# Retention attention and a gated feed-forward layer on one core: the first load on two queues, the last unit and the last output rows in two parts, and a new table of priority shifts

## The chip, the cores and the metric

The kernel runs on one core of a Trainium2 chip. A core has five engines that run side by side, each through its own list of instructions in order: PE (TensorE, matrix products), DVE (VectorE), ACT (ScalarE), POOL (GpSimd) and SP (SyncE, which here only issues transfers). Engines wait for each other by semaphores. Transfers are issued by SP or ACT and carried by 16 DMA engines. The metric is device time in microseconds (us), less is better.

## The reference, cut to what matters

```python
# q, k, v: (4, 8, 768, 64); per head: decayed attention in blocks, with a carried state
intra = einsum('bhic,bhjc->bhij', qb, kb) * Dmask       # lam ** (i - j), lower triangle
out   = einsum('bhij,bhjd->bhid', intra, vb) + einsum('bhid,bhde->bhie', qb * lam_pow, kv_state)
kv_state = lam_block * kv_state + einsum('bhsd,bhse->bhde', kb * rev_pow, vb)
# x: (3072, 512), heads side by side
xn = x / sqrt(mean(x * x) + 1e-6) * rms_g
g  = xn @ w_gate                                          # 512 x 1536
y  = (g * sigmoid(g) * (xn @ w_val)) @ w_out              # 1536 x 512
```

All tensors are float32.

## The kernel before, in words

The 3072 tokens are six groups `m` of 512 (four tiles `t` of 128), the heads four pairs `p`, and the 1536 hidden columns twelve slices `f` of 128. For each group and pair PE computes scores (`pa`, L509), sums for the state (`pst`, L542), the mix of values (`po`, L574) and the state's part (`po`, L585); ACT scales K with the decay (L519), DVE multiplies the scores with the mask (L529) and carries the state (L555, L557), POOL scales Q (L533). A group's rows are then normalised: row sums on PE (`pss`), a power on POOL, spread by PE (`pr`), a product on DVE (L716), a 16-bit cast on ACT (L721) and the rest of it on DVE or POOL (L724).

A unit `u` is one slice of one group in the feed-forward layer. It makes gate and value products (`pg` and `pv`, L763, in the first groups; `pa` and `pb`, L938, seven products instead of eight, later), SiLU on ACT, `mul_sums` on DVE (L1004), `high` on ACT (a 16-bit cast, L1028) and `low` on DVE (the rest, L1035). Then `out_product` adds three products to each of the four accumulators `acc` (L782 to L784). After the last slice `out_rows` scales an accumulator into a tile `o` and `send` stores it.

float32 weights arrive as raw 64-bit words (`raw_gv` gate and value, `raw_o` output rows) and are converted on the chip: lift (ACT, L220), shifts (DVE, L229 and L232), squares (ACT, L442) whose sums are a product on PE (`pn`, L447), and the 16-bit high and low parts (`wg`, `wv`, L465 and L469). The first weight tile lands in `partial`.

Constants `cs` (lambda and rms_g) come in one small transfer. DVE makes decay masks and powers from them (scans, L156 and L161), and `gmax`, the largest rms_g, which PE spreads (`pmax`, L185).

All order is written by a planner. Every step is given an engine, a cost, a due time `at` in units and what it reads and writes; `SHIFTS` adds an amount to the due time of the steps that it names by number; `Plan.run` then plays the steps through on a clock of its own and emits them in the order that comes out, engine by engine, loads and stores (on SP) included. Where that clock leaves PE idle by more than 0.8 in the beginning, `busy` puts unread products there (`unread`, L144). Loads of Q, K, V and of gate and value weights share four buffers, tag `in`, so each waits until an older tile is no longer used; `pending` is the order in which they are asked for.

Of the kernel before, what the change touches and what calls it, by code (L numbers as in the profile page):

```python
# [17 lines left out]
P = 128  # L18
G = 512
# [4 lines left out]
def retention_swiglu_kernel(  # L24
# [50 lines left out]
    nc.sync.dma_start(cs, consts)  # L75
# [6 lines left out]
    def load_qkv(m, p):  # L82
        t = stage.tile([P, 4, GC, P], F32, tag="in", name=f"qkv_{m}_{p}", bufs=4)
        for i in range(2):
            queue = nc.scalar if m == p == i == 0 else nc.sync
            queue.dma_start(
                t[:, 2 * i : 2 * i + 2],
                qkv[m, p, :, 2 * i : 2 * i + 2].rearrange("p a (c i) -> p a c i", c=GC),
            )
        loaded[m, p] = [t[:, i] for i in range(4)]  # L90
# [699 lines left out]
    def out_rows(m, f, t, kept, half):  # L790

        acc = done_accs.pop((m, f, t))
# [13 lines left out]
        if m == NG - 1 and t == GC - 1:  # L806

            o = tmp.tile([P, DM], F32, tag="t", name=f"o_{m}_{t}")
            left, right = slice(0, DM // 2), slice(DM // 2, DM)
            copy(o[:, left], acc[:, left], False)  # L810
            nc.sync.dma_start(rows_[:, left], o[:, left])
            copy(o[:, right], acc[:, right], True)
            nc.scalar.dma_start(rows_[:, right], o[:, right])
            return
# [13 lines left out]
    def send(m, t):  # L828
        rows_, o = outs.pop((m, t))
        nc.sync.dma_start(rows_, o)  # L830
# [112 lines left out]
    class Hidden:  # L943
# [59 lines left out]
        def mul_sums(self):  # L1003
            nc.vector.scalar_tensor_tensor(  # L1004
                self.sg, self.val, cv[:, self.f : self.f + 1], self.sg, ALU.mult, ALU.mult
# [15 lines left out]
        def high(self):  # L1021
            if self.half:
# [3 lines left out]
            else:  # L1026
                self.hh = hp.tile([P, G], F32R, tag="hh", name=f"hh_{self.m}_{self.f}")
            nc.scalar.copy(self.hh, self.sg)  # L1028

        def low(self):  # L1030
# [319 lines left out]
    def out_steps(u, h, ats):  # L1350
# [4 lines left out]
        for t, at in enumerate(ats):  # L1355
            r = [f"hh{u}", weights] + ([] if h.half else [f"hl{u}"])
# [7 lines left out]
            ends = m == NG - 1 and t == GC - 1  # L1364
            tag = "t" if ends else "o" if t < GC - 1 else "w"
            r = [f"{acc}_{t}"] + ([f"partial:{t}"] if m == 0 else []) + (["ik"] if h.half else [])
            step("DVE" if m == 0 or t % 2 == 0 else "ACT", 0.74, at - 0.5, out_rows, m, f, t, m == 0, h.half,
                 r=r, w=[f"o{m}_{t}"], new=[(f"o{m}_{t}", tag)])
            if not ends:
                step("ST", 0.05, at, send, m, t, r=[f"o{m}_{t}"], w=[f"sent{m}_{t}"], lasts=4.0)  # L1370
# [69 lines left out]
    def arrive_steps():  # L1440
# [3 lines left out]
        step("LD", 3.4, -9, arrive, w=["cs"])  # L1444
        step("LD", 0.1, -9, arrive)
        for p in range(NP):
            for c in ("qK", "kv"):
                step("LD", 1.45, -9, arrive, w=[f"q0_{p}:{x}" for x in c])
# [114 lines left out]
    def strassen(u, h):  # L1563
# [25 lines left out]
        step("DVE", 0.42, u - 1, h.sum_val, 1, 1, r=[b, "kept0:1"], w=["kept1:1"])  # L1589
        step("DVE", 0.78, u - 0.9, h.mul_sums, r=["kept1:0", "kept1:1", "cv"], w=[f"sg{u}:0", f"sg{u}:1"])  # L1590
        tag = ("hh", "hl")[f % 2]
# [23 lines left out]
    def load_steps():  # L1615
# [204 lines left out]
```

## Time and profile before

| what | us |
|---|---|
| median of 3 runs (lowest to highest) | 660.43 (660.37 to 660.57) |
| the profiled execution | 659.59 |
| its span, first to last instruction | 657.8 |
| PE busy | 650.3 (99%) |
| DVE busy | 425.0 (65%) |
| ACT busy | 335.5 (51%) |
| POOL busy | 151.3 (23%) |
| last store issued, from the span's start | 654.50 |

The profile is of one execution. Times in it count from the span's start. A row of instructions gives start, duration, engine, line, operation, output and input tiles (numbers of buffers left out), shapes, and in brackets how long the engine stood idle before and what ended that. An x with a number counts records; a float32 product leaves two records. A PE record lasts longer than the step to the next start, because products overlap. Line numbers are those of the kernel before; in the kernel after, the same code stands 3 to 10 lines lower (L509 becomes L512, L763 becomes L766, L782 becomes L785).

### The profile page before, as it was taken

To read this page: it belongs to the slowest core of one execution; us is meant where nothing else is said; L and a number is where in the kernel's file an instruction comes from. 1 tells how busy PE (TensorE), PEld (TensorE's weight loads), DVE (VectorE), ACT (ScalarE), POOL (GpSimd) and SP (SyncE) were. 2 spreads that over 40 slices of the span, in tenths; PEclk is the share of its full clock that TensorE was granted. 3 is DMA by queue.
4 is the path that set the end of the run, shared out by engine and by line. 5 is a ranking of instruction groups with operands and counts; after the bars stand their busy time and mean duration, and the time that the engine had idled before them with its cause. 6 is when DMAs were issued, how large, how long until landed. Compare 5 with 4: busy or idle time off the path is not lost.

```text
span 657.8 us, 12390 instructions
## 1 busy us (share of the span) xinstructions
PE 650.3 (99%) x5049; PEld 442.4 (67%) x5049; DVE 425.0 (65%) x823; ACT 335.5 (51%) x674; POOL 151.3 (23%) x133
## 2 busy tenths in 40 slices
PE   9999999999999999999999999999999999999997
PEld 8845655554665556677767777777777777777774
DVE  6798898779987666866574434487443488443333
ACT  3795867658754553455454434445444335433332
POOL 2201250001475654477220011003010102000000
PEclk9999999999999999999999999999999999999999
DMA  8818654411013010112100311100230000000001
GB/s 322 338 48 316 239 210 162 162 64 59 8 64 126 24 45 1 65 66 65 65 2 1 127 67 65 65 2 1 73 122 1 1 2 1 33 33 1 1 1 64
DMA packets 14313, 51.13 MB, mean 78 GB/s; under 512 B 1712, under 2 KB 1968, under 8 KB 12848
## 3 DMA queue, kind: packets, MB, share of 16 engines
q1 hardware_dynamic: 13968, 49.69, 20.8%
q8 instruction: 39, 0.64, 0.4%
q10 hardware_dynamic: 288, 0.66, 0.4%
q14 instruction: 18, 0.15, 0.1%
HBM read 44.05 MB, written 6.29 MB: 77 GB/s over the span
## 4 chain that ended last, share of the span: by engine, by line
PE 96%; DVE 2%; ACT 1%; issue 0%; POOL 0%; DVEq 0%; POOLq 0%
PE pa L938 19%; PE pb L938 14%; PE acc L782 10%; PE pv L763 10%; PE pg L763 9%; PE acc L784 9%; PE acc L783 9%; PE pa L509 4%; PE po L574 4%; PE po L585 3%; PE pst L542 2%; PE unread L144 1%; PE pss L630 1%; DVE hh L1035 1%; PE pr L663 0%; DVE sg L1004 0%
## 5 line engine op out<-in xcount | busy, mean ns | idle before, releaser
L986 ACT COPY tx<-pa 128x256 f32<-128x256 f32 x144 | 53.6, 372 | 136.4 <-PE pa L938 135.7
L784 PE MATMUL acc<-wo,hh 128*128 128x512 f16 (+1 forms) x288 | 110.3, 383 | 0.0
L783 PE MATMUL acc<-wo,hh 128*128 128x512 f16 (+1 forms) x288 | 110.2, 383 | 0.0
L990 DVE TENSOR_TENSOR tx<-pb,tx 128x256 f32<-128x256 f32 x96 | 40.8, 425 | 73.6 <-PE pb L938 65.2
L782 PE MATMUL acc<-wo,hh 128*128 128x512 f16 x216 | 82.3, 381 | 0.7 <-DVE hh L1035 0.7
L938 PEld LDWEIGHTS <-wo 128*128 128x128 f16 x576 | 56.1, 98 | 26.6 <-issue 1.3
L994 DVE TENSOR_TENSOR sg<-pb,tx 128x256 f32<-128x256 f32 x48 | 20.3, 424 | 77.7 <-ACT tx L986 77.6
L763 PE MATMUL pv<-x,wv 128*128 128x512 f16 x288 | 69.5, 379 | 0.0
L763 PE MATMUL pg<-x,wg 128*128 128x512 f16 x288 | 69.0, 380 | 0.0
L938 PEld LDWEIGHTS <-wg 128*128 128x128 f16 x576 | 56.4, 98 | 16.1
L938 PEld LDWEIGHTS <-wv 128*128 128x128 f16 x576 | 56.3, 98 | 6.9 <-issue 0.2
L1028 ACT CAST hh<-sg 128x512 f16<-128x512 f32 (+1 forms) x72 | 44.5, 618 | 31.2 <-DVE sg L1004 16.4
L533 POOL TENSOR_TENSOR qkv<-qkv,pw 128x512 f32<-128x512 f32 x24 | 31.3, 1303 | 101.9 <-PE pa L509 67.5
L763 PEld LDWEIGHTS <-wg 128*128 128x128 f16 x288 | 26.1, 98 | 33.5 <-issue 3.6
L763 PEld LDWEIGHTS <-wv 128*128 128x128 f16 x288 | 26.7, 98 | 32.3 <-issue 2.8
L1035 DVE TENSOR_TENSOR hh<-sg,hh 128x512 f16<-128x512 f32 x54 | 42.3, 784 | 4.7 <-ACT hh L1028 2.2
L1004 DVE SCALAR_TENSOR_TENSOR sg<-tx,cv,sg 128x512 f32<-128x512 f32 x48 | 38.3, 797 | 5.0
L938 PE MATMUL pb<-tx,wo 128*128 128x256 f16 x288 | 39.3, 273 | 0.6 <-DVE tx L990 0.6
L938 PE MATMUL pa<-x,wv 128*128 128x256 f16 x288 | 39.3, 273 | 0.0
L938 PE MATMUL pa<-tx,wo 128*128 128x256 f16 x288 | 39.3, 273 | 0.0
L938 PE MATMUL pb<-x,wg 128*128 128x256 f16 x288 | 39.3, 273 | 0.0
L938 PE MATMUL pa<-x,wg 128*128 128x256 f16 x288 | 39.3, 273 | 0.0
(180 smaller groups left out, 1151.8 us busy)
## 6 DMA issues: line engine op xcount, KB each, us to landing
qkv<-in_qkv_dram SPq DMA_DIRECT2D x47, 512.0 KB, 4.9
raw_gv<-in_weights_dram SPq DMA_DIRECT2D x11, 1024.0 KB, 7.4
raw_o<-in_weights_dram SPq DMA_DIRECT2D x12, 512.0 KB, 3.7
out_dram<-o SPq DMA_DIRECT2D x23, 256.0 KB, 2.1
partial<-in_weights_dram SPq DMA_DIRECT2D x2, 512.0 KB, 11.9
qkv<-in_qkv_dram ACTq DMA_DIRECT2D x1, 512.0 KB, 4.6
out_dram<-o SPq DMA_DIRECT2D x1, 128.0 KB, 1.7
out_dram<-o ACTq DMA_DIRECT2D x1, 128.0 KB, 2.4
```

The source lines that it names most:

```text
L509: nc.tensor.matmul(self.pa[j][:, c, :], self.kT[r, c, :], self.qT[r, c, :], start=True, stop=True,)
L533: eng.tensor_mul(self.qT, self.qT, pw[:, p : p + 1, :].broadcast_to([P, GC, P]))
L763: nc.tensor.matmul(ps, w[:, kk, :], x[:, kk, :], start=i == kk == 0, stop=i == 2 and kk == NK - 1,)
L782: nc.tensor.matmul(acc, hl[:, ts_], oh, start=first, stop=False)
L783: nc.tensor.matmul(acc, hh[:, ts_], ol, start=False, stop=False)
L784: nc.tensor.matmul(acc, hh[:, ts_], oh, start=False, stop=last)
L938: nc.tensor.matmul(ps, w(ow, k), x(ox, k), start=first and i == k == 0, stop=i == 2 and k == 1, skip_group_check=True,)
L986: nc.scalar.copy(self.kept[:, i], self.pa)
L990: nc.vector.tensor_add(self.val[:, half], self.pb, self.kept[:, i])
L1004: nc.vector.scalar_tensor_tensor(self.sg, self.val, cv[:, self.f : self.f + 1], self.sg, ALU.mult, ALU.mult)
L1028: nc.scalar.copy(self.hh, self.sg)
L1035: nc.vector.tensor_sub(self.hl, self.sg, hh)
```

## The change

1. **First load.** The first half (Q and K) of pair 0 of group 0 was one transfer on ACT's queue; it becomes two, token tiles 0 and 1 on ACT's queue and 2 and 3 on SP's. `cs` moves from the front of SP's queue to the second place on ACT's, and the other half (K and V) from SP's queue to the third place on ACT's.
2. **Order of loads.** Group 1's second pair is asked for ahead of the second weight tile, and later loads shift.
3. **Last unit.** `mul_sums`, `high` and `low` of the last unit work in two halves of 256 tokens, so that accumulators 0 and 1 wait for the first half only.
4. **Last rows.** The last output tile was made half by DVE and half by ACT, and sent by SP and by ACT; now DVE makes both halves in two small tiles, and SP sends both. Tile 2 of the last group moves from DVE to ACT (`scalar_copies`).
5. **Planner.** A new table of shifts, new costs of the first arrivals, and fewer unread products: the planned idle time is divided by 0.4 and not by 0.24.

```diff
     cs = const.tile([P, NC], F32, name="cs")
-    nc.sync.dma_start(cs, consts)
...
-        for i in range(2):
-            queue = nc.scalar if m == p == i == 0 else nc.sync
-            queue.dma_start(
-                t[:, 2 * i : 2 * i + 2],
-                qkv[m, p, :, 2 * i : 2 * i + 2].rearrange("p a (c i) -> p a c i", c=GC),
-            )
+        rows_ = qkv[m, p].rearrange("p a (c i) -> p a c i", c=GC)
+        if m == p == 0:
+            nc.scalar.dma_start(t[:, :2, : GC // 2], rows_[:, :2, : GC // 2])
+            nc.sync.dma_start(t[:, :2, GC // 2 :], rows_[:, :2, GC // 2 :])
+            nc.scalar.dma_start(cs, consts)
+            nc.scalar.dma_start(t[:, 2:], rows_[:, 2:])
+        else:
+            for i in range(0, 4, 2):
+                nc.sync.dma_start(t[:, i : i + 2], rows_[:, i : i + 2])
...
-    pending = [(load_qkv, 1, 0), (load_gv, 1)]
-    for i in range(1, NP):
-        pending += [(load_gv, i + 1), (load_qkv, 1, i)]
+    pending = [
+        (load_qkv, 1, 0), (load_qkv, 1, 1), (load_gv, 1), (load_gv, 2),
+        (load_qkv, 1, 2), (load_gv, 3), (load_gv, 4), (load_qkv, 1, 3),
+    ]
...
-        if m == NG - 1 and t == GC - 1:
-
-            o = tmp.tile([P, DM], F32, tag="t", name=f"o_{m}_{t}")
-            left, right = slice(0, DM // 2), slice(DM // 2, DM)
-            copy(o[:, left], acc[:, left], False)
-            nc.sync.dma_start(rows_[:, left], o[:, left])
-            copy(o[:, right], acc[:, right], True)
-            nc.scalar.dma_start(rows_[:, right], o[:, right])
+        if part is not None:
+            o = tmp.tile([P, DM // 2], F32, tag="t", name=f"o_{m}_{t}_{part}")
+            cols = slice(part * DM // 2, (part + 1) * DM // 2)
+            copy(o, acc[:, cols], False)
+            outs[m, t, part] = rows_[:, cols], o
             return
...
-            copy(o, acc, t % 2)
+            copy(o, acc, scalar_copies(m, t))
...
+    def scalar_copies(m, t):
+        return m > 0 and t in ((1, 2) if m == NG - 1 else (1, 3))
...
+        if u == len(units) - 1:
+            for i in range(2):
+                step("DVE", 0.46, u - 0.9 + 0.1 * i, h.mul_sums, i, r=[f"kept1:{i}", "cv"], w=[f"sg{u}:{i}"])
+                step("ACT", 0.39, u + 0.2, h.high, i, r=[f"sg{u}:{i}"], w=[f"hh{u}:{i}"],
+                     new=[] if i else [(f"hh{u}", tag)])
+                step("DVE", 0.42, u + 0.3, h.low, i, r=[f"sg{u}:{i}"], w=[f"hh{u}:{i}"])
+            return
...
-        56: 1.6, 82: 1.1, 93: 1.5, 112: 2.05, 114: 0.25, 116: 0.3, 131: -2.4, 137: -17.9,
+        57: 1.25, 61: 1.5, 63: 2.1, 64: 1.65, 67: 2.95, 69: 0.25, 70: 3.05, 73: 3.4, 86: -0.25,
...
-                    busy(int((idle - 0.3) / 0.24))
+                    busy(int((idle - 0.2) / 0.4))
```

What this makes of the instruction lists, at the places that the prediction speaks of. PE at the start, before: `unread` are the unread products, `pa` scores, `pst` state sums, `po` the mix of pair 0.

```order
L144 MATMUL unread_152<-ident 128x128 x13
L509 MATMUL pa_0_0_166<-qkv_0_97 128x128
L509 MATMUL pa_0_1_167<-qkv_0_97 128x128
L144 MATMUL unread_185<-ident 128x128 x4
L542 MATMUL pst_0_190<-qkv_0_97 64x64 x8
```

PE at the start, after:

```order
L147 MATMUL unread_148<-ident 128x128 x5
L188 MATMUL pmax<-ident,gmax 128x128
L512 MATMUL pa_0_0_163<-qkv_0_96 128x128
L512 MATMUL pa_0_1_164<-qkv_0_96 128x128
L147 MATMUL unread_178<-ident 128x128 x3
L545 MATMUL pst_0_182<-qkv_0_96 64x64 x8
L512 MATMUL pa_1_0_192<-qkv_1_101 128x128
```

The scores have four such pairs of products each time. `pmax`, which came after the scores of pair 1, now stands ahead of the first scores, and the scores of pair 1 ahead of the mix of pair 0.

SP's first transfers, before (`qkv_0` to `qkv_3` are first the pairs of group 0; after `partial`, those of group 1):

```order
L75 DMA cs<-in_consts_dram 128x16
L86 DMA qkv_0_97<-in_qkv_dram 128x1024
L86 DMA qkv_1_100<-in_qkv_dram 128x1024 x2
L98 DMA partial<-in_weights_dram 128x1024 x2
L86 DMA qkv_0_333<-in_qkv_dram 128x1024 x2
L101 DMA raw_gv_372<-in_weights_dram 128x2048
L107 DMA raw_o_401<-in_weights_dram 128x1024
L101 DMA raw_gv_422<-in_weights_dram 128x2048
L107 DMA raw_o_448<-in_weights_dram 128x1024
L86 DMA qkv_1_477<-in_qkv_dram 128x1024 x2
```

SP's first transfers, after:

```order
L86 DMA qkv_0_96<-in_qkv_dram 128x2x256
L91 DMA qkv_1_101<-in_qkv_dram 128x1024 x2
L100 DMA partial<-in_weights_dram 128x1024 x2
L91 DMA qkv_0_330<-in_qkv_dram 128x1024 x2
L91 DMA qkv_1_360<-in_qkv_dram 128x1024 x2
L103 DMA raw_gv_398<-in_weights_dram 128x2048
L109 DMA raw_o_430<-in_weights_dram 128x1024
L103 DMA raw_gv_454<-in_weights_dram 128x2048
L109 DMA raw_o_480<-in_weights_dram 128x1024
L91 DMA qkv_2_489<-in_qkv_dram 128x1024 x2
```

`cs` and one half of pair 0 have left SP's queue, a quarter of pair 0 has come, and pair 1 of group 1 (`qkv_1_360`) stands ahead of the second weight tile (`raw_gv_398`).

PE around the first gate products, before (`pr` spreads the row scales, `pn` are the weights' norm products, `pg` and `pv` gate and value of slice 0; weight loads between the products are not shown):

```order
L663 MATMUL pr_466<-ident,y_443 128x128 x4
L447 MATMUL pn_0_481<-ssq_445,ones_b 128x1
L585 MATMUL po_0_456<-qkv_0_333,state 64x128 x6
L144 MATMUL unread_515<-ident 128x128 x6
L447 MATMUL pn_1_522<-ssq_445,ones_b 128x1
L763 MATMUL pg_0_526<-x_248,wg 128x512
L763 MATMUL pv_0_536<-x_248,wv 128x512
L509 MATMUL pa_1_0_568<-qkv_1_477 128x128
```

and after:

```order
L588 MATMUL po_0_437<-qkv_0_330,state 64x128 x6
L666 MATMUL pr_466<-ident,y_452 128x128 x4
L147 MATMUL unread_501<-ident 128x128 x8
L766 MATMUL pg_0_510<-x_243,wg 128x512
L450 MATMUL pn_0_517<-ssq_498,ones_b 128x1
L766 MATMUL pv_0_539<-x_243,wv 128x512
L450 MATMUL pn_1_548<-ssq_498,ones_b 128x1
```

Before, both `pn` stood ahead of the gate products, of which four were followed by four value products; now four gate products, `pn_0`, the other eight, and then the value products, with no scores (`pa_1`) among them.

DVE at the very end, before:

```order
L1004 SCALAR_TENSOR_TENSOR sg_11_6844<-tx_2433,cv,sg_11_6844 128x512
L1035 TENSOR_TENSOR hh_11_6871<-sg_11_6844,hh_11_6871 128x512
L800 TENSOR_SCALAR o_0_6883<-acc_0_0_6183,ik 128x512
L800 TENSOR_SCALAR o_2_6894<-acc_0_2_6214,ik 128x512
L800 TENSOR_SCALAR o_3_6897<-acc_0_3_6219,ik 128x256
```

and after:

```order
L1009 SCALAR_TENSOR_TENSOR sg_11_6834<-tx_2385,cv,sg_11_6834 128x256 x2
L1039 TENSOR_TENSOR hh_11_6859<-sg_11_6834,hh_11_6859 128x256 x2
L803 TENSOR_SCALAR o_0_6876<-acc_0_0_6173,ik 128x512
L803 TENSOR_SCALAR o_3_0_6890<-acc_0_3_6209,ik 128x256
L803 TENSOR_SCALAR o_3_1_6893<-acc_0_3_6209,ik 128x256
```

`o_2` has gone to ACT, and the last unit's two steps and the last rows come in halves.

More of the change, by code (lines that the diff above doesn't have):

```diff
@@ L788, in retention_swiglu_kernel, with out_rows @@
     done_accs = {}
-    def out_rows(m, f, t, kept, half):
-        acc = done_accs.pop((m, f, t))
+    def out_rows(m, f, t, kept, half, part=None):
+        acc = done_accs[m, f, t]
         def copy(o, ps, on_scalar):
@@ L1019, in mul, with high @@
             )
-        def high(self):
-            if self.half:
+        def high(self, t=None):
+            half = slice(0, G) if t is None else slice(t * HG, (t + 1) * HG)
+            if self.half and not t:
                 tag = ("hh", "hl")[self.f % 2]
@@ L1025, in high, with low @@
                 self.hh, self.hl = both[:, 0], both[:, 1]
-            else:
+            elif not self.half:
                 self.hh = hp.tile([P, G], F32R, tag="hh", name=f"hh_{self.m}_{self.f}")
-            nc.scalar.copy(self.hh, self.sg)
-        def low(self):
+            nc.scalar.copy(self.hh[:, half], self.sg[:, half])
+        def low(self, t=None):
+            if t is not None:
+                half = slice(t * HG, (t + 1) * HG)
+                nc.vector.tensor_sub(self.hl[:, half], self.sg[:, half], self.hh[:, half])
+                return
             hh = self.hh
```

36 lines of the change are left out of this document (22 added, 14 removed), and 46 rows, old and new, of the table SHIFTS.

## The prediction

> **What bounds the kernel now.** I read, in this order, the page's busy shares, the span, the table of stages, who waits for whom on PE (TensorE), and then the first 40 and last 10 us instruction by instruction.
>
> ```profile
> PE   650.3 (99%) x5049; PEld 442.4 (67%) x5049; DVE 425.0 (65%) x823; ACT 335.5 (51%) x674; POOL 151.3 (23%) x133
> core 0: 657.8 us, clock 1.000
> 0.00:30.00 30.00, 28.25 (x358) 25.35 (x359) 20.55 (x60) 15.31 (x32) 8.46 (x15) 1.00 0.89 335
> 30.00:100.00 70.00, 69.98 (x464) 41.09 (x463) 62.71 (x115) 51.66 (x95) 17.38 (x13) 1.00 0.56 210
> PE acc L782 <- DVE hh L1035: 0.5, 1, 0.5
> PE pb L938 <- DVE tx L990: 0.6, 1, 0.6
> ```
>
> In each stage row the first number after the stretch is its length, the second PE's busy time, the fourth DVE's (VectorE), the last what DMA moved in GB/s. PE is the bound from end to end: 7.5 us of 657.8 are idle, two waits of 0.5 and 0.6 us in the long middle, the rest at the ends. So only four things can move the time: unproductive PE time in the first 33 us, the cost of PE's own order, waits in the middle, and what follows the last product.
>
> The sum below is made against the profiled execution (659.59 us, span 657.8); the median of the runs is 660.43, 0.84 above it, and the differences are carried over to the median.
>
> **First stage.** The rows are start, duration, engine and operation; of the DMA rows the last number is us from issue to landing.
>
> ```profile
> 1.47 4.96 PE L144 MATMUL unread<-ident 128*128 128x128 f32 x26 [1.47 <-POOL ident masks.py:199]
> 0.74 0.41 ACTq L86 DMA_DIRECT2D qkv<-in_qkv_dram  x1
> qkv<-in_qkv_dram ACTq DMA_DIRECT2D x1, 512.0 KB, 4.6
> cs<-in_consts_dram SPq DMA_DIRECT2D x1, 8.0 KB, 3.8
> qkv<-in_qkv_dram SPq DMA_DIRECT2D x1, 512.0 KB, 5.4
> 4.57 0.16 DVE L178 TENSOR_REDUCE gmax<-cs 128x1 f32<-128x4 f32 x1 [4.57 <-DMA cs<-in_consts_dram]
> 6.36 1.16 PE L509 MATMUL pa<-qkv 64*128 64x128 f32 x16
> 6.66 0.91 ACT L519 ACTIVATE qkv<-qkv,mask 128x256 f32<-128x256 f32 x2 [3.78 <-DVE pw L161]
> 7.45 1.16 PE L144 MATMUL unread<-ident 128*128 128x128 f32 x8
> 7.55 1.29 DVE L529 TENSOR_TENSOR a<-pa,mask 128x512 f32<-128x512 f32 x2
> 8.54 0.69 PE L542 MATMUL pst<-qkv 128*64 128x64 f32 x16
> 12.34 0.69 PE L542 MATMUL pst<-qkv 128*64 128x64 f32 x16
> 26.33 0.65 ACT L442 ACTIVATE junk<-w 128x512 bf16<-128x512 f32 x1
> 31.14 2.58 ACT L721 CAST x<-xn 128x512 f16<-128x512 f32 x4
> 33.22 1.13 PE L763 MATMUL pg<-x,wg 128*128 128x512 f16 x4
> 34.43 0.74 DVE L469 SCALAR_TENSOR_TENSOR wg<-w,sc,wg 128x512 f16<-128x512 f32 x1
> ```
>
> Q and K of pair 0 land at 0.74 + 4.6 = 5.34, but the 13 unread matmuls (26 records) hold PE until 6.4: an overrun of 1.05 us, the most that thinning them can give here. Eight later records take 8.54 - 7.45 = 1.09, 0.136 each; the first 26 average 0.191, as if 10 ran at 0.272 (half speed) and 16 at 0.136. Five matmuls are ten records: 1.47 + 2.7 = 4.2. PE then waits, since the new order puts pmax ahead of the scores and pmax needs gmax, hence cs. cs loses its place at the front of SP's queue and stands second on ACT's, behind 256 KB. No row shows that; it lands no earlier than before (0.74 + 3.8 = 4.54) and, as 8 KB, hardly after the 5.34 of the 512 KB that stood there. I take 5.1, nearer the later end, because 512 KB (both halves) now move ahead of it. Then gmax 0.16, pmax some 0.4 and handovers: scores at 5.8 instead of 6.4.
>
> Half of that is not kept. DVE ran nine scans from 4.64 to 7.55 (0.32 each) before the first decay of the scores; now seven, from about 5.2, so it starts at 7.45, 0.1 earlier. The K and V half of pair 0 moves from SP's second place (landing 1.17 + 5.4 = 6.57) to ACT's third, sharing the engines with pair 1: I take 7.2, between 6.57 (no earlier than it was) and 8.1 (512 KB of pair 1 ahead of it, at the 335 GB/s of the first stage row). ACT's 0.91 brings the first state sums to 8.2 against 8.54; the three unread matmuls ahead of them lie in that wait and cost nothing. Pair 1's scores need both decays (7.45 + 1.29); from there PE runs through, and the state sums of pair 1 come at about 11.6 instead of 12.34: 0.7 ahead.
>
> By the first gate product less is left. The new order does a row sum and the scores of group 1 ahead of pair 3's last product, so by PE's rows added up in that order the last row sum ends about 0.1 earlier only; and it puts norm product pn_0 between the first 4 and the next 8 of pg_0, while ACT's order has pn_0's square behind the four casts (31.14 + 2.58 = 33.7, and 0.65 with its read-out): PE, whose old order had value products there, waits some 0.4. Against that, DVE finishes the low halves some 0.7 earlier, since the 0.74 for the first gate's weights moves ahead of the normalisation. I take **-0.3** for the stage, between -1.05 (the overrun) and +1.5 (a rival below).
>
> Group 1's second pair now loads ahead of the second weight tile, whose buffer is now pair 2's, free at about 20.9 (PE's rows added up from 11.6), not pair 1's.
>
> ```profile
> raw_gv<-in_weights_dram SPq DMA_DIRECT2D x1, 1024.0 KB, 5.1
> raw_gv<-in_weights_dram SPq DMA_DIRECT2D x1, 1024.0 KB, 11.4
> ```
>
> It lands at 20.9 + 5.1 = 26.0 by the row issued when the queue had emptied. ACT's new order has a square, a copy, two decays and a cast (0.5 to 0.65 each) between pair 3's output, at about 25.5, and its lift, so at 28: hidden, with 2 us of cover. What queues behind it on SP (the next tiles) is needed later still.
>
> **PE's order.** Attention products (pa, pst, po) are cut into fewer runs between the 16-bit ones.
>
> ```profile
> 38.58 1.04 PE L763 MATMUL pg<-x,wg 128*128 128x512 f16 x4
> 39.54 0.71 PE L509 MATMUL pa<-qkv 64*128 64x128 f32 x8
> 40.19 1.04 PE L763 MATMUL pv<-x,wv 128*128 128x512 f16 x4
> 41.06 1.89 PE L763 MATMUL pg<-x,wg 128*128 128x512 f16 x8
> ```
>
> Four gate products followed by an attention run take 39.54 - 38.58 = 0.96 from start to start, four followed by their like 41.06 - 40.19 = 0.87: 0.1 per change. Counted in the two orders after the first gate product, 61 such changes become 56: **-0.5**, all on PE's path. From about 280 us on PE's order is the same.
>
> **Middle.** The wait of 0.6 is at 339.4, where all orders are the same: it stays. The 0.5 at 207 lies where they differ; it may go (-0.5), and new ones may come: DVE is busy 62.71 of 70 us at 30:100 and steps move there. Other steps moved by the table swap places under a busy PE: nothing as long as DVE and ACT keep ahead. I take **0**, from -0.5 to +1.2 (two waits like the longest seen).
>
> **End.**
>
> ```profile
> 647.95 0.42 DVE L990 TENSOR_TENSOR tx<-pb,tx 128x256 f32<-128x256 f32 x1 [1.77 <-PE pb L938]
> 648.48 0.75 DVE L1004 SCALAR_TENSOR_TENSOR sg<-tx,cv,sg 128x512 f32<-128x512 f32 x1
> 650.12 0.38 PE L784 MATMUL acc<-wo,hh 128*128 128x512 f16 x1
> 650.66 0.39 PE L782 MATMUL acc<-wo,hh 128*128 128x512 f16 x1 [0.16 <-DVE hh L1035]
> 652.17 0.69 ACT L798 ACTIVATE o<-acc,ik 128x512 f32<-128x512 f32 x1 [2.29 <-PE acc L784]
> 652.81 1.14 DVE L800 TENSOR_SCALAR o<-acc,ik 128x512 f32<-128x512 f32 x2 [0.54 <-PE acc L784]
> 653.04 0.38 PE L784 MATMUL acc<-wo,hh 128*128 128x512 f16 x1
> 654.50 0.35 ACTq L813 DMA_DIRECT2D out_dram<-o  x1
> out_dram<-o SPq DMA_DIRECT2D x1, 128.0 KB, 1.7
> out_dram<-o ACTq DMA_DIRECT2D x1, 128.0 KB, 2.4
> ```
>
> Products start 0.215 apart, so PE could go on at 650.33 and waits for the last low half until 650.66. Product, cast and low half go in two parts of 256 columns, 0.42 each by the row of that width: the first part is through at 648.48 + 3 x 0.42 = 649.74, the second 0.42 later at 650.16, and the 0.33 goes. Last product 652.71 + 0.38 = 653.09. ACT copies t=1 until 652.54 and now t=2 until 653.25; SP issues it at 653.28 (0.43). DVE does the last row's halves (0.39 each, from the 1.14 less 0.75) to 653.91; SP issues them at 653.71 and 654.04. By SP's 1.7 the last lands at 655.75, by ACTq's 2.4 at 656.45; before, 654.50 + 2.4 = 656.9. I take 1.9, nearer SP's row since it is that queue, with a little for the store ahead: **-0.95** (-1.15 to -0.45), the 0.33 included.
>
> **Sum.** -0.3 - 0.5 + 0 - 0.95 = -1.75: 660.43 becomes about 658.7. 0.2% is 1.3 us, about what a measurement of this kernel tells from no change.
>
> **Rivals.**
> - *The first half lands no earlier.* For it: until 4 us the ACT load had the DMA engines almost to itself, as the two rows below (3.0 to 3.5 us: packets, MB, share) show. Against: from 4.0 SP's packets took half. Stage 0 instead of -0.3: 659.0. The Trainium skill, "DMA: Bandwidth & Descriptors", Rules for kernel authors, speaks for this: spreading DMAs over SP and ACT brings no bandwidth, since all run on the same 16 engines. By that rule the sum is -1.45; the rows agree up to 4 us.
>
> ```profile
> q10 hardware_dynamic: 27, 0.11, 114.4%
> q1 hardware_dynamic: 4, 0.00, 0.5%
> ```
>
> - *PE is still slow when the data come.* Ten records of work end at 4.2, about where the old ones became fast, and PE then idles a microsecond. If the speed stays halved, pmax, scores and three unread matmuls (2.3 us) take twice as long, of which the wait for the state sums hides 0.5 (8.2 less 5.4 + 2.3): 1.8 on top of -0.3, +1.5, total +0.05, 660.5. The granted clock reads 1.00 throughout, so only durations can show it. The Trainium skill, "TensorE: Matmul & The Clock Gate", Part 1, says that full clock needs about 3.4 us of sustained work in a free-running window; the 26 records (about 2.8 us slow) agree roughly, and by it 2.7 us of work may fall short.
> - *DVE becomes late after the first gates:* two new waits of 0.6, total -0.55, 659.9.
> - *Slower:* the second weight tile lands late. Should it take the 11.4 of the row above, it lands at 32.3, 4 us past the lift's turn on ACT at 28; the first gate's later products wait behind pn_0, and +4 - 1.75 = +2.25, 662.7. It decides from a landing of about 31 on; a queue that has emptied by 20 us speaks against it.
> - *More:* the wait at 207 goes and the whole overrun is won: -3.0, 657.4.
>
> **Chances.** Forecast 0.46, no earlier landing 0.10, slow PE 0.13, late DVE 0.15, slower 0.06, more 0.10. The first, the last and most of the landing case are faster by over 0.2%: 0.62; slow PE, late DVE and the rest are within it: 0.31; slower 0.07. The range 657.3 to 660.6 takes in all but the slower case and the edges.
>
> **What would show it.** First L512 row at about 5.8 (a start after 6.3: cs or the clock; records over 0.2 there: the clock); second L545 group near 11.6; first L766 row before 33.2; no PE wait on DVE between 33 and 300 us; no wait at the last unit's first acc product; last store on SP near 654.0. I am wrong if PE's idle time in the middle grows by over 1 us, or if the first gate comes after 33.5.

## The result, and the profile after

The changed kernel is slower: 671.08 us, median of six runs (669.32 to 674.72), against 660.40 for the kernel before beside it on the same chip. The ratio is 1.0170, 95% interval 1.0144 to 1.0196, so about 11 us; the forecast was 658.7, its range 657.3 to 660.6. Two single runs far above their like, one of e9 (742.67) and one of the kernel before beside e15 (1743.83), are in no ratio below.

The page after, its span and the busy shares:

```profile
span 669.4 us, 12356 instructions
PE 651.3 (97%) x5029; PEld 441.8 (66%) x5029; DVE 423.4 (63%) x825; ACT 335.6 (50%) x675; POOL 155.7 (23%) x133
```

The table of stages after (length, then busy time of PE, PEld, DVE, ACT, POOL, the granted clock, DMA share, GB/s):

```profile
0.00:30.00 30.00, 25.03 (x310) 21.53 (x311) 17.51 (x48) 12.14 (x25) 7.17 (x14) 1.00 0.82 293
30.00:100.00 70.00, 67.57 (x465) 40.87 (x465) 59.88 (x119) 51.41 (x94) 18.34 (x14) 1.00 0.57 206
100.00:200.00 100.00, 100.00 (x518) 57.00 (x518) 83.43 (x164) 67.72 (x125) 26.94 (x23) 1.00 0.25 85
200.00:260.00 60.00, 60.00 (x419) 32.57 (x418) 39.73 (x75) 27.76 (x51) 37.09 (x32) 1.00 0.21 71
260.00:300.00 40.00, 34.16 (x322) 23.92 (x320) 29.26 (x56) 17.32 (x39) 21.39 (x18) 1.00 0.17 54
300.00:640.00 340.00, 339.26 (x2834) 249.12 (x2832) 182.93 (x346) 149.34 (x324) 44.81 (x35) 1.00 0.10 35
```

One row of the same table before, which the prediction did not show:

```profile
260.00:300.00 40.00, 40.00 (x353) 28.55 (x351) 28.09 (x53) 20.14 (x48) 23.19 (x21) 1.00 0.19 64
```

PE does the same work (651.3 us, 650.3 before) and stands idle in three stretches: 3.2 us more before 30, 2.4 more from 30 to 100, 5.8 more from 260 to 300. The rest is as before. Who PE waits for longest, after, once its unread products have begun (us in total, times, longest):

```profile
PE pmax L188 <- DVE gmax L181: 3.5, 1, 3.5
PE pa L941 <- DVE a L532: 2.8, 1, 2.8
PE acc L785 <- DVE hh L1045: 2.1, 2, 1.5
PE pn L450 <- DVE a L532: 1.3, 1, 1.3
```

Before, once the unread products had begun, PE had no wait over 0.6 us. The rows of the first stage after, as the prediction showed them of before (start, duration, engine):

```profile
1.47 2.50 PE L147 MATMUL unread<-ident 128*128 128x128 f32 x10 [1.47 <-POOL ident masks.py:199]
7.23 0.16 DVE L181 TENSOR_REDUCE gmax<-cs 128x1 f32<-128x4 f32 x1 [7.23 <-DMA cs<-in_consts_dram]
7.44 0.80 PE L188 MATMUL pmax<-ident,gmax 128*128 128x128 f32 x2 [3.47 <-DVE gmax L181]
8.16 2.08 PE L512 MATMUL pa<-qkv 64*128 64x128 f32 x16
9.87 0.91 ACT L522 ACTIVATE qkv<-qkv,mask 128x256 f32<-128x256 f32 x2 [5.92 <-DMA qkv<-in_qkv_dram]
15.53 0.69 PE L545 MATMUL pst<-qkv 128*64 128x64 f32 x16
35.87 0.90 PE L766 MATMUL pg<-x,wg 128*128 128x512 f16 x2
```

And its first transfers, with KB and us from issue to landing:

```profile
qkv<-in_qkv_dram ACTq DMA_DIRECT2D x1, 256.0 KB, 4.9
qkv<-in_qkv_dram SPq DMA_DIRECT2D x1, 256.0 KB, 4.6
qkv<-in_qkv_dram ACTq DMA_DIRECT2D x1, 512.0 KB, 8.0
cs<-in_consts_dram ACTq DMA_DIRECT2D x1, 8.0 KB, 6.0
```

The constants land at 7.23 instead of 4.57, the scores start at 8.16 instead of 6.36 and take 2.08 instead of 1.16, the second state product comes at 15.53 instead of 12.34, the first gate at 35.87 instead of 33.22: 2.65 us late. The halves of Q and K land at 5.6 and 5.3, where the whole landed at 5.34; K and V, which ScalarE's decay waits for, only at 9.87.

The wait of 1.3 us for the mask product, at 53.0, has a chain behind it that the profile follows back to a weight tile, the third of those that go to `raw_gv`. It was asked for at 39.94 (30.48 before), ScalarE's lift waited for it, and the VectorE steps that end with the mask product stand behind that lift:

```profile
45.60 1.15 ACT L223 ACTIVATE w<-raw_gv 128x1024 f32<-128x1024 f32 x1 [1.16 <-DMA raw_gv<-in_weights_dram]
53.00 0.16 PE L450 MATMUL pn<-ssq,ones_b 128*128 128x2 bf16 x1 [1.32 <-DVE a L532]
```

No run changes the place of this tile alone, so what it costs by itself is not shown.

The end, after (last product, last rows, issue of the last five stores, and how long the last two take to land):

```profile
664.94 0.38 PE L787 MATMUL acc<-wo,hh 128*128 128x512 f16 x1
665.36 0.88 DVE L803 TENSOR_SCALAR o<-acc,ik 128x256 f32<-128x256 f32 x2 [1.19 <-PE acc L787]
664.19 2.56 SPq L833 DMA_DIRECT2D out_dram<-o  x5
out_dram<-o SPq DMA_DIRECT2D x2, 128.0 KB, 2.1
```

The last product starts 11.9 us later than before (664.94, 653.04) and the end comes 4.46 us behind it instead of 4.76; the wait at the last unit is gone. So the tail did what it was to do, and the loss lies ahead of it: about 2.65 by the first gate, some 2.4 of idle time from there to 100, and the jump of 5.8 from 260 to 300.

### The profile page after: what moved, and what is told of

The parts are those of the page before. It is cut to its first block, busy times and chain, and to the rows that moved or that the text cites. A ratio compares the mean times of both kernels' runs of the same rounds, so it can differ in the third digit from the quotient of the medians.

```text
span 669.4 us, 12356 instructions
## 1 busy us (share of the span) xinstructions
PE 651.3 (97%) x5029; PEld 441.8 (66%) x5029; DVE 423.4 (63%) x825; ACT 335.6 (50%) x675; POOL 155.7 (23%) x133
## 4 chain that ended last, share of the span: by engine, by line
PE 88%; DVE 5%; issue 2%; POOL 2%; DMA 2%; ACT 0%; ACTq 0%; DVEq 0%; POOLq 0%; SPq 0%
PE pa L941 18%; PE pb L941 14%; PE acc L785 10%; PE acc L787 9%; PE acc L786 9%; PE pv L766 8%; PE pg L766 8%; PE pa L512 4%; PE po L577 3%; PE po L588 3%; PE pst L545 2%; PE pss L633 1%; DMA cs<-in_consts_dram 1%; DMA raw_gv<-in_weights_dram 1%; DVE x L727 1%
## 5 line engine op out<-in xcount | busy, mean ns | idle before, releaser
L1034 ACT CAST hh<-sg 128x512 f16<-128x512 f32 (+2 forms) x73 | 44.7, 612 | 30.0 <-DVE sg L1009 14.7
L1045 DVE TENSOR_TENSOR hh<-sg,hh 128x512 f16<-128x512 f32 x53 | 40.6, 766 | 4.9 <-ACT hh L1034 2.2
L1009 DVE SCALAR_TENSOR_TENSOR sg<-tx,cv,sg 128x512 f32<-128x512 f32 (+1 forms) x49 | 38.0, 776 | 4.9
L941 PE MATMUL pb<-x,wv 128*128 128x256 f16 x288 | 39.3, 273 | 0.0
```

What stands on the lines that cost most here:

```text
L941: nc.tensor.matmul(ps, w(ow, k), x(ox, k), start=first and i == k == 0, stop=i == 2 and k == 1, skip_group_check=True,)
L1009: nc.vector.scalar_tensor_tensor(sg, self.val[:, half], cv[:, self.f : self.f + 1], sg, ALU.mult, ALU.mult)
L1034: nc.scalar.copy(self.hh[:, half], self.sg[:, half])
L1045: nc.vector.tensor_sub(self.hl, self.sg, hh)
```

## The experiments

Every run has the kernel before beside it on the same chip; the interval is of the ratio to it. Traces are of one execution each, and the same first stage can differ by 0.7 us between two of them: the first gate of e3, whose first stage is that of the kernel before, came at 33.89 and not at 33.22.

| run | us | before | ratio, 95% |
|---|---|---|---|
| changed kernel | 671.08 | 660.40 | 1.0170 (1.0144-1.0196) |
| e1 changed, load as before | 667.95 | 659.89 | 1.0128 (1.0105-1.0152) |
| e2 before, new load | 664.83 | 659.89 | 1.0068 (1.0055-1.0082) |
| e3 before, new tail | 659.45 | 659.89 | 0.9993 (0.9984-1.0002) |
| e4 changed, more warm-up | 670.91 | 659.89 | 1.0165 (1.0151-1.0179) |
| e5 before, new load, K/V on SP | 664.81 | 660.26 | 1.0068 (1.0045-1.0090) |
| e6 before, new load, constants first | 660.19 | 660.26 | 0.9999 (0.9990-1.0009) |
| e7 changed, four entries out | 665.42 | 660.26 | 1.0082 (1.0065-1.0099) |
| e8 changed, load as before, entries from 900 out | 660.87 | 660.26 | 1.0009 (0.9992-1.0026) |
| e9 as e8, more warm-up | 660.80 | 660.23 | 1.0007 (0.9998-1.0016) |
| e10 before, pair ahead | 663.05 | 660.23 | 1.0051 (1.0032-1.0069) |
| e11 changed, constants first, four entries out | 662.39 | 660.23 | 1.0033 (1.0019-1.0046) |
| e12 changed, mask product moved | 671.86 | 660.23 | 1.0177 (1.0163-1.0191) |
| e13 changed, scores moved | 672.00 | 659.73 | 1.0188 (1.0172-1.0203) |
| e14 changed, one entry out | 665.60 | 659.73 | 1.0090 (1.0073-1.0106) |
| e15 changed, scores and sums moved | 675.28 | 659.77 | 1.0235 (1.0216-1.0253) |
| e16, e17 changed, third unit ahead too | 674.71, 673.67 | 660.21 | 1.0228 (1.0190-1.0266), 1.0205 (1.0187-1.0222) |

### The load, undone and alone

e1 puts `cs` and `load_qkv` of the kernel before into the changed one; e2 puts the new ones into the kernel before.

> The changed kernel with the first load as before (constants first on SP's queue, Q and K whole on ACT's, K and V whole on SP's); its order of work, warm-up and tail stay. Theory H (two separate losses: 2.65 us up to the first gates because the constants land at 7.23 instead of 4.54 us, and some 9 us later that the new order makes by itself): 668 to 669 us, first gates near 33.3 us, the idle of 2.8 us at 294 and the POOL wait of 8.5 us before 280 stay. Theory L (all of it follows from the late start, since the engines' queues fall out of step): 659 to 661 us and no wait over 1 us between 260 and 300.

> The kernel before with only the first load changed (halves of Q and K over two queues, constants behind the first half on ACT's queue); order, warm-up and tail as before. Theory H: the constants land near 7.2 us, the masks are 2.7 us later, the first scores are not held by them in this order: first gates 1.5 to 2.7 us later, time 662 to 663. Theory L: a late start alone brings the later losses too: 668 to 671. Rival (what costs is only that the maximum of the constants stands ahead of the scores in the new order): 660 to 661.

e1: 667.95, so the load costs 3.1 us by the medians (2.8 by the ratios) and 8 stay, with the waits of 2.8 and 2.1 us where they were: theory H. Its first gate came at 32.96. e2: 664.83, 4.9 slower, more than theory H gave (662 to 663) and without any later loss: against theory L too. The order of before, in which the maximum of the constants does not stand ahead of the scores, is hurt as well. PE of e2:

```profile
6.59 1.16 PE L511 MATMUL pa<-qkv 64*128 64x128 f32 x16
10.95 1.02 PE L544 MATMUL pst<-qkv 128*64 128x64 f32 x15 [2.11 <-ACT qkv L521]
13.98 2.08 PE L511 MATMUL pa<-qkv 64*128 64x128 f32 x16
17.21 0.69 PE L544 MATMUL pst<-qkv 128*64 128x64 f32 x16
38.09 1.13 PE L765 MATMUL pg<-x,wg 128*128 128x512 f16 x4
```

The scores start at 6.59, no earlier than the 6.36 of before; the first state product is 2.4 us late, after an idle time of 2.1 the next scores run at half speed (2.08), and the 4.87 us at 17.21 are still there at the first gate (38.09 against 33.22) and, by the medians, at the end. There is no slack in this stretch. The start of the scores does not test the halves here: the 13 unread products of the old order hold PE until about 6.6.

Two transfers had been put back in the queue, the constants and the K and V half. e5 and e6 part them (the edits are against e2):

```diff
 e5:         nc.scalar.dma_start(cs, consts)
-            nc.scalar.dma_start(t[:, 2:], rows_[:, 2:])
+            nc.sync.dma_start(t[:, 2:], rows_[:, 2:])
 e6: (cs first on SP's queue, as before)
-            nc.scalar.dma_start(cs, consts)
```

> The kernel before with halves of Q and K over two queues and the constants behind the first half on ACT's queue, but K and V of that pair on SP's queue, as before. The whole new load alone cost 4.9 us (664.83). Theory K (what costs is K and V third on ACT's queue: ScalarE's decay began at 10.4 instead of 6.66 us, the first state product at 10.95 instead of 8.54, and the clock went cold meanwhile): 660 to 661, state product at 8.5 to 9.2. Theory C (what costs is the constants, at 7.2 instead of 4.57 us): 663.5 to 665, for the masks come no earlier than in the run with the whole new load.

> The kernel before with halves of Q and K over two queues, K and V behind the first half on ACT's queue, but the constants first on SP's queue, as before. Theory K: K and V land near 9.5 us still, state product near 10.5, time 663 to 665. Theory C: 659.5 to 660.5. If the halves themselves help, the first scores start before 6.36 us; in the run with the whole new load they started at 6.59.

e5 664.81, e6 660.19: theory C. With the constants first, halves and K and V on ACT's queue cost nothing and bring nothing in the old order; with the constants behind half a load, K and V in their old place do not help. In e6 the first half did land earlier, 4.1 us after the start instead of 5.34, but the unread products held the scores until 6.92. VectorE of e5, and GpSimd:

```profile
6.64 0.16 DVE L180 TENSOR_REDUCE gmax<-cs 128x1 f32<-128x4 f32 x1 [6.64 <-DMA cs<-in_consts_dram]
7.67 0.72 DVE L158 TENSOR_TENSOR_SCAN mask<-cs,ident 128x128 f32<-128x128 f32 x2
8.62 1.75 DVE L158 TENSOR_TENSOR_SCAN mask<-cs,ident 128x128 f32<-128x128 f32 x2
10.61 1.26 DVE L531 TENSOR_TENSOR a<-pa,mask 128x512 f32<-128x512 f32 x2
8.62 1.47 POOL L535 TENSOR_TENSOR qkv<-qkv,pw 128x512 f32<-128x512 f32 x1 [7.02 <-PE pa L511]
```

The path is constants, scans for the masks, mask product. The constants are 2.07 late (6.64 against 4.57), the mask product 3.06 (10.61 against 7.55): two scans that take 0.72 alone fall beside GpSimd's multiplication and take 1.75. The Trainium skill, "Trainium Architecture — The Big Picture", What this means for kernel authors, says that VectorE and GpSimd share a pair of ports under an exclusive lock; these rows agree: the scans lose 1.03 us beside the 1.47 that GpSimd works.

e4 keeps PE busy until the constants come: `busy(int((idle - 0.2) / 0.4) + 11 * (now == 1.5))`.

> The changed kernel with 16 instead of 5 warm-up products ahead of the first real one, so that PE is not idle from 3.97 to 7.43 us; they compute nothing that is used. If the slow records after that idle time (first scores 2.08 us for 16 records instead of 1.16, then 1.65 instead of about 0.75 for 6) cost the head: pa 0 at 1.1 us and second state product near 14.0 instead of 15.5, time 669.5 to 670.2. Rival (the masks, which wait for the constants, hold the chain anyway, or later slack takes it up): 671.

670.91: no gain that can be told. The scores ran at full speed:

```profile
7.79 1.16 PE L512 MATMUL pa<-qkv 64*128 64x128 f32 x16
11.03 1.08 PE L545 MATMUL pst<-qkv 128*64 128x64 f32 x16 [1.21 <-ACT qkv L522]
14.96 0.69 PE L545 MATMUL pst<-qkv 128*64 128x64 f32 x16
```

But PE then waited 1.21 for ScalarE's decay of K, and of the 3.2 us at the second state product only 0.57 came back. So the slow records of the changed kernel lay beside another wait, for K and V. The Trainium skill, "TensorE: Matmul & The Clock Gate", Part 1, explains the speed (some 3.4 us of sustained work first); the row agrees, with 5.4 us of unread products ahead of it. It did not move the time.

### The order: one entry of the table

e7 takes the last four entries out of `SHIFTS`; e8 has the first load as before and no entry from step 900 on (38 of them).

```diff
-        1033: -0.85, 1056: 4.25, 1061: 0.8, 1064: 0.8, 1077: -4.9, 1079: -4.1, 1083: -4.1,
-        1084: -4.1,
+        1033: -0.85, 1056: 4.25, 1061: 0.8, 1064: 0.8,
```

> The changed kernel without the last four entries of its table (steps 1077, 1079, 1083, 1084, which pull four products of the first 16-bit unit of the next group 4.1 to 4.9 units ahead); all else stays. Theory S (these four make the idle time of 5.8 us between 260 and 300): 665.3 to 667, and no wait over 1 us there. Rival (VectorE and GpSimd are full there, whatever PE does first, and the time is lost at another place): 670 to 671.

> The changed kernel with the first load as before (alone 667.95) and without the entries of its table from step 900 on (38 of them). Theory S (the late entries make the 5.8 us between 260 and 300, the early ones 2.4 us of waits from 37 to 53): 661.5 to 662.5. Rival (the pair loaded ahead of the second weight tile is what puts the later stages out of step): 666 to 668.

> The changed kernel with one entry of its table out, that of step 1083 (the sixth product of the next group's first unit, pulled 4.1 units ahead). The program is instruction for instruction that of the run without the last four entries (665.42): the other three move nothing. So this is a second sample of it, beside the run above on the same chip: 664.8 to 666.4. Rival (the earlier run's 5.7 us was the chip of that hour): 668 to 671.

e7 665.42, 5.7 less than the changed kernel: theory S. e14 keeps three of the four entries, is the same program, and gave 665.60. So one number of this table, -4.1 for step 1083 (one 16-bit product of 0.66 us), costs 5.5 to 5.7 us. The stage row of e7:

```profile
260.00:300.00 40.00, 38.48 (x365) 28.21 (x364) 28.95 (x54) 19.72 (x45) 16.07 (x13) 1.00 0.15 54
```

And what PE still waits for longest in it from 250 to 300:

```profile
PE acc L785 <- DVE hh L1045: 0.6, 1, 0.6
PE po L577 <- ACT sq L611: 0.6, 1, 0.6
```

The waits of 2.84 and 1.48 us are gone, 4.3 in all, and nothing takes their place: this part of the loss is the order's, and it is not one that a late start brought. e8: 660.87, no different from before and 0.6 below what theory S gave; its stage row has no idle time left there:

```profile
260.00:300.00 40.00, 40.00 (x383) 29.48 (x381) 28.45 (x55) 20.55 (x49) 26.05 (x25) 1.00 0.27 91
```

Two rows of its PE, the first gate and the longest wait behind it:

```profile
31.44 0.90 PE L764 MATMUL pg<-x,wg 128*128 128x512 f16 x2
48.06 0.16 PE L448 MATMUL pn<-ssq,ones_b 128*128 128x2 bf16 x1 [0.78 <-DVE a L530]
```

In this profile the new early order brings the first gate 1.8 us ahead of before (31.44 against 33.22) and gives it back in 1.9 us of idle time from 30 to 50 us, the longest wait 0.78. The same weight tile stands at the start of that wait as in the changed kernel: asked for at 35.51, ScalarE waits 0.61 for it. e9 adds warm-up products to e8.

> The kernel of the run without the late entries (first load as before, no entries from step 900 on; 660.87, from 658.2 to 663.7) with 13 instead of 5 warm-up products, as many as the kernel before has. Theory W (with constants and data early, PE meets its first products on a slow clock: first scores 1.86 us instead of 1.16 and the pieces behind them slow too): 659.5 to 660, and less spread between runs. Rival (the products come when the data do, and the slow records lie beside ScalarE's decay): 660.9.

660.80: the rival; the spread did narrow (ten of its eleven runs from 660.1 to 661.3, against 658.2 to 663.7). e11 tests whether the two losses add up.

> The changed kernel with two things undone: the constants go first on SP's queue (the halves of Q and K and the place of K and V stay as changed), and the last four entries of the table are out. If the two losses found (3.1 us by the load, 5.7 us by the four entries) are separate and the halves cost nothing: 662 to 662.7. Rival (they overlap, or the halves cost something in this order): 664 to 666.

662.39, as expected from 671.08 - 3.1 - 5.7 = 662.3: they are separate. Of the 2.2 us left over before, its profile, of a run 1.4 us above the median, shows two stretches of idle time, 2.0 us from 20 to 100 (0.3 before) and 1.5 from 260 to 300, with the tail's 0.4 against them; that makes 2.8, so the sizes fit only roughly. It also shows what the halves do in the new order: the first half lands at 3.9, the scores start at 4.33, PE waits 0.40 for the other half and 1.11 for the decay of K, and the first state product comes at 8.48, where before had it at 8.54.

### How that entry costs: not isolated

Five kernels keep the table and move steps by hand between 275 and 300 us, where the first units of the group that starts at 268 run. e12 moves the mask product of pair (3,2), on which PE waits 2.84, ahead of VectorE's weight sums; e13 moves that pair's scores behind the third unit's products; e15 the weight sums of tiles 8 and 9 too; e16 and e17 bring four products of the third unit ahead of the second unit's output, without and with the sums. All do it in this way, with other numbers:

```diff
         order = plan.run()
+        moved = {i: (t, i) for t, i in order if i in (1183, 1215, 1216)}
+        order = [x for x in order if x[1] not in moved]
+        at = [i for _, i in order].index(1144)
+        order[at:at] = [moved[i] for i in (1215, 1216, 1183)]
```

> The changed kernel with its table whole, and three steps put in another place of the order: the two products of pair (3,2)'s scores with the mask on VectorE ahead of the weight sums of tile 8, and GpSimd's first addition for tile 9 behind them (it takes the second of two buffers which these scores need). PE's order stays. Theory M (PE's 2.84 us at 294 is the wait for that mask product, which stands behind sums that wait for GpSimd): this wait falls below 0.5, time 668 to 669. Rival (what is put off then holds the next unit's weights, and the time is lost there): 670.5 to 671.5.

> The changed kernel with its table whole, but the scores of pair (3,2) and what reads them (the two products with the mask on VectorE, GpSimd's decay of that pair's queries) moved behind the third unit's products, to about the place they have with the four entries out; the fifth unit's first product, which needs the same bank, moves behind the fourth unit's. In the changed kernel these scores stand ahead of the third unit and hold its two banks until VectorE has read them: PE waits 2.84 us at 294. Theory B (this place of the scores is what the four entries cost): the wait is gone, 665.5 to 668. Rival G (GpSimd and VectorE reach the weight sums too late for the third unit, whatever holds the banks): another wait of 2 us or more stands there instead, 670 to 671.5, as with the mask product moved alone (671.86).

> The changed kernel with its table whole; in the order, the weight sums of tile 8 (two steps on VectorE, three on ScalarE, three on GpSimd) and then the scores of pair (3,2) with what reads them stand behind the third unit's products, and the weight sums of tile 9 and GpSimd's additions for tile 10 behind the fourth unit's. In the changed kernel VectorE comes to the sums of tile 8 at 289.7 and of tile 9 at 296.1, each time after waiting for GpSimd's last low part of the tile before (one buffer), and the third unit's own steps are queued behind them. Theory G (it is these sums ahead of the third unit's steps that cost): 665.5 to 667.5, and no wait over 1 us on PE from 286 to 298. Rival B' (the order of PE around 275 to 286 costs, whatever stands on VectorE): 670.5 to 672, as in the two runs that moved less.

> The changed kernel with its table whole, the scores of pair (3,2) moved behind the third unit's products as in the run that gave 672.0, and four of the third unit's products (with what keeps them on ScalarE and VectorE) moved ahead of the second unit's output products. In the changed kernel and in the two runs that moved less, PE comes from the second unit's last product straight to its output products and waits 1.5 to 2.1 us for VectorE's low half; without the four entries the third unit's products stand in between. Theory F (cover: PE needs those products there): this wait is gone, 668 to 670; what stays is VectorE's sums of tiles 8 and 9 ahead of the third unit's later steps. Rival (the wait moves on as before): 671 to 673.

> As the run beside it, and the weight sums of tiles 8 and 9 and GpSimd's additions for tile 10 later too, as in the run that gave 675.28. Theory F with G (cover for the second unit's split, and the sums out of the way of the third unit): 666 to 668. Rival (each hand-made move makes a new wait further on, and only an order planned as a whole gives the 5.7 us back): 671 to 675.

671.86, 672.00, 675.28, 674.71, 673.67: none gave anything back, and the last three cost 2.6 to 4.2 us more. The rivals had the direction right each time, but four of the five came out above the range that the rival gave, e15 by 3.3 us. PE's waits in e12 tell how:

```profile
PE pb L941 <- DVE sg L997: 2.3, 1, 2.3
PE acc L785 <- DVE hh L1045: 2.3, 2, 1.7
```

And one row of its VectorE:

```profile
296.70 0.43 DVE L888 TENSOR_TENSOR ws<-r 128x256 f32<-128x256 f32 x1 [3.29 <-POOL wg L910]
```

The wait for `a` is gone, and 2.3 us of wait for `sg` stand in its place, for VectorE, its queue in order, now waits 3.29 for GpSimd's weight sums. PE's idle time from 250 to 300 was 5.81 us in it and 5.84 in the changed kernel. VectorE's weight sums ahead of `a` are not the answer either: in the changed kernel two of them fall beside GpSimd's work and take 1.47 and 1.37 us, 0.42 alone, which is 2.0 of the 2.84; in e12 they take 0.42 and the time is no shorter. So it is shown that the entry costs 5.5 to 5.7 us and that taking away the longest wait that it leaves gives nothing back; which of the reordered steps would have to move together stays open.

### The pair ahead of the weight tile

e10 changes only SP's list in the kernel before (group 1's second pair in second place): `pending[1:4] = [pending[i] for i in (3, 1, 2)]`.

> The kernel before with one thing changed: group 1's second pair is loaded from the second place of SP's list (where the second weight tile stood), the second and third weight tile one place later; the other engines' order stays. Theory P (the second weight tile, issued near 23 instead of 16.1 us, lands near 28 to 30, and ScalarE, which takes it up at 25.8, holds what is queued behind it): 663.5 to 665. Rival (the buffers and the slack of the first gates take it up): 660 to 661.

663.05, 2.8 us slower, a little under what theory P gave. ScalarE and PE of e10:

```profile
28.87 0.66 ACT L220 ACTIVATE w<-raw_gv 128x512 f32<-128x512 f32 x1 [2.23 <-DMA raw_gv<-in_weights_dram]
31.53 0.16 PE L447 MATMUL pn<-ssq,ones_b 128*128 128x2 bf16 x1 [2.60 <-DVE a L529]
```

ScalarE waits 2.23 for the tile and PE 2.60 behind it. In the changed kernel ScalarE's order takes that tile later, at 31.90, and does not wait for it (issued at 25.00): there it is hidden. The tile that is not hidden there is the one asked for at 39.94.

### The tail alone

e3 has the changed kernel's last unit, last rows and `scalar_copies` in the kernel before.

> The kernel before with only the end changed (last unit's product and its split in two halves, last output rows in two parts on VectorE and SP's queue, ScalarE copying rows 1 and 2). From the two traces (0.3 us of wait at 650.7 gone, 4.08 instead of 4.38 us from the last product's end to the end): 659.8, 0.6 below before. The prediction's term was 0.95: 659.5. Rival (the end is set by how long the last stores take, whatever feeds them): 660.4.

659.45 against 659.89, ratio 0.9993: the size fits the 0.6 of the traces, and the interval (1.1 us faster to 0.1 slower) does not part it from nothing. It is the fastest of all these kernels, and not measurably faster than the one before.

## Why the prediction was wrong, point by point

**First stage, -0.3 (from -1.05 to +1.5): wrong, +2.65.** The step that failed is "I take 5.1" for the constants. It was bounded by 5.34, the landing of 512 KB that had had the DMA engines nearly to itself; in the new load two queues carry Q and K, each half lands at 5.3 to 5.6, and the constants behind them at 7.23. "Scores at 5.8" became 8.16, the second state product "about 11.6" 15.53. A second term was off too: K and V, "I take 7.2", at most 8.1, came at 9.87; in the old order their place cost nothing (e6). The order's own part was there: with the load as before the first gate came at 32.96 (e1), 31.44 (e8) and 32.59 (e9), ahead of the 33.22. The rival "the first half lands no earlier", given 0.10, was right in the changed kernel (5.6), not with the constants out of that queue (4.1 in e6, 3.9 in e11), and there the time did not gain by it. The Trainium skill, "DMA: Bandwidth & Descriptors", Rules for kernel authors, had been cited for it; in halves, Q and K as a whole came no sooner (5.0 to 5.8 us in the profiles with halves, 4.7 to 5.3 in those without), which agrees. The rival "PE is still slow" was right in its rows (2.08, 1.65 for six) and wrong in its price (e4). What the prediction lacked is the combination: constants that land late delay VectorE's scans, the masks and all that follows, and none of the cases had that.

**Second weight tile.** "Hidden, with 2 us of cover" held in the changed kernel's own order; its issue came at 25.00, not 20.9, the first stage being late. "What queues behind it on SP (the next tiles) is needed later still" did not hold: the third `raw_gv` tile was asked for at 39.94, ScalarE waited 1.16 us for it, and PE's 1.3 at 53.0 hang on it by the profile's chain. The rival's mechanism, a late second tile, costs 2.8 us in the old order (e10), where it was priced at 4 in the new one.

**PE's order, -0.5:** neither shown nor refuted; whatever it is worth is smaller than the waits that came with it.

**Middle, 0 (from -0.5 to +1.2): wrong.** Most of what the load leaves of the miss lies here: 5.5 to 5.7 us by one entry (e14, e7) and some 1.7 between 20 and 100 in e11. The step that failed is "nothing as long as DVE and ACT keep ahead", with "two waits like the longest seen" as its bound. The longest wait of the old order says nothing of the new one: no row of the trace of before bounds it. The order near 260 to 300 had changed on PE, VectorE and GpSimd, the scores of pair (3,2) standing ahead of the third unit there, and was not followed through. "From about 280 us on PE's order is the same" is a misreading: those scores stand in one piece at 283.92 before and in two, at 279.74 and 285.79, after, and the orders of PE come together again only at that pair's mix of values, at 294.31 and 306.26.

**End, -0.95 (from -1.15 to -0.45):** right in sign and mechanism, too large. The wait of 0.3 went as said; of the 0.62 for the stores 0.3 came (landing 2.1 us after issue, not 1.9, and five issues on SP one behind the other). e3 has 0.44.

**The chances.** 0.07 for slower was too little for a change that replaced the order of most of the program. Two of the signs of being wrong that it named came true: PE's idle time in the middle grew by over 1 us, and the first gate came after 33.5.

## What to carry to other kernels

The smallest transfer on which the first arithmetic depends goes first on its queue; splitting the large one over two queues gained no time in any run here, putting 8 KB behind 256 KB cost 3 to 5 us in a stretch without slack. When an order is replaced as a whole, its waits can't be bounded by those of the old one: either follow the new order engine by engine, loads included, or give the slow side a large chance. And the wait that the profile names is where a bad order shows, not necessarily what to move: five moves that each took the named wait away, or tried to, gave none of the 5.7 us back, while taking out one number did.

## What the hardware showed unexpectedly

- A small transfer went with slow neighbours on its queue. K and V (512 KB) landed 8.0 to 8.7 us after issue behind half a load and the 8 KB of constants (changed kernel, e2, e4, e7, e14), 5.6 and 6.6 us behind the half alone (e6, e11); that half took 4.3 to 5.0 us with the constants behind it and 3.4 and 3.2 without. Why is not shown. The constants themselves took 1.6 us (e11) to 3.8 us (before) at the front of SP's queue, and 5.4 to 6.3 behind 256 KB (e5, e2, e4, e14, changed kernel, e7). Of e2, with KB and us to landing:

```profile
qkv<-in_qkv_dram ACTq DMA_DIRECT2D x1, 512.0 KB, 8.5
cs<-in_consts_dram ACTq DMA_DIRECT2D x1, 8.0 KB, 5.7
```

  And of e6, where the 8 KB are out of that queue:

```profile
qkv<-in_qkv_dram ACTq DMA_DIRECT2D x1, 512.0 KB, 5.6
cs<-in_consts_dram SPq DMA_DIRECT2D x1, 8.0 KB, 1.8
```

- PE fell back to half speed after 2.1 us without work (e2: 16 records in 2.08 us, 1.16 at full speed; the granted clock read 0.50 from 14 to 16 us). In the changed kernel the scores took the same 2.08 us at 8.16, after 3.47 without work, and the granted clock from 8 to 10 read 1.00: at the start of a trace only the durations show a slow PE. A wait may cost twice in this way: in e1's profiled run, 671.28 and the slowest of its four, output products took 0.63 us instead of 0.40 after a wait of 1.45, with 0.66 as the clock from 50 to 55.
